# RWKV-7 attention with a SoLU block: wider inverse steps for the first six groups, narrower couplings, a new order for the first slots

## The chip, the cores and the metric

The kernel runs on one core of one Trainium2 chip, as one launch. The metric is the device time in microseconds (us). The core has five engines with a queue of instructions each: TensorE (PE in the profile, its weight loads PEld), VectorE (DVE), ScalarE (ACT), GpSimd (POOL) and SyncE (SP), which only issues transfers.

## The reference

```python
# attention: r, k, v, w, a, b are [4, 8, 768, 40]
state = zeros(B, H, 40, 40)
for t in range(768):
    y[:, :, t] = einsum('bhd,bhde->bhe', r_t, state)
    Sa = einsum('bhde,bhe->bhd', state, a_t)
    state = state * w_t[:, :, None, :] - einsum('bhd,bhe->bhde', Sa, b_t) + einsum('bhd,bhe->bhde', v_t, k_t)
x = y.transpose(0, 2, 1, 3).reshape(3072, 320)
# block: w_in [320, 1024], w_out [1024, 320] (float64), g_ln [1024]
h = x @ w_in
e = exp(h - max(h)); sm = e / (sum(e) + 1e-9)
solu = h * sm
out = ((solu - mean(solu)) / sqrt(var(solu) + 1e-6) * g_ln) @ w_out
```

All of it is float32 in the kernel; the float64 weights are taken apart by bit operations on the chip.

## The kernel before

The sequence is cut into 12 chunks of 64 tokens, and the four batches into two pairs, which makes 24 slots (slot i is pair i % 2 of chunk i // 2). In a slot the recurrence is solved in closed form: within a chunk every token depends on earlier ones through a strictly triangular 64 x 64 matrix per head, one for each of 16 heads of a pair. This matrix is cut in two halves of 32 (Q = 32). Its two diagonal 32 x 32 blocks are inverted on VectorE; the block off the diagonal is put together from these by two rounds of small products on TensorE, the coupling and the closing.

The steps of a slot, with the names that stand in the order list:

- w, b, a, k, v, r load the inputs (names with the slot's number). lg, Tc, xi, xe, sb, sk scale them with the running decay; sb and sk are VectorE's instructions "kb". Ta, Tb, Tk, Tv, Tr, Tei are transposes on TensorE, Ea, Eb, Ekv, Er, Eei their evictions (Ea is VectorE's "aT").
- N builds the triangular matrices, nt evicts them, sn stores their diagonal blocks to DRAM.
- Z, B, i: the inversion, done for two slots at once (GRP = 2), so there are 12 groups. B brings 64 blocks (two slots by two halves by 16 heads) onto 128 partitions as the tile blk, each block twice, for two sets of 16 columns. The pieces i0.1 to i0.30 are the 30 steps j of group 0: step j adds row j of blk, times column j of the result uu, to the columns behind it. U stores uu to DRAM, tu and uh bring the two diagonal inverses of a slot into the tiles tu and uh.
- F flips a tile, C (coupling) multiplies by the off-diagonal matrix nt, wy is its eviction, D (closing) multiplies by uh, and tl evicts the result into the tile tu.
- Sk, Sv, mk, mv are scores and their masks; K, V and x0 build the right side from the state, S solves with tu, clu and mlu evict and mask it as lu. R0, R1 read the answers; t, ks, an keep the state and write the answer x; lv and l move x through DRAM into xT, for h two slots later.
- H0 to H4 are h = x @ w_in, m the row maximum (the tile nmax), e, we, sq, rs the softmax and the norm, Te and Ee a transpose, P, Pr, Eo and So the product with w_out and its store.
- nb, ns, nf split the float64 weights in three stages (13 pieces: 5 of w_in, 8 of w_out), L lands them, g loads g_ln, and Tmean0 to Tmean2 with "centre" take the mean out of w_out.

An inverse step before (lines 548 to 564) depends on j. n_c = (j + 1) // 2 columns are live, and m = 31 - j elements are behind. For n_c under 4 there is one scalar_tensor_tensor per column (line 552). Else the columns are split in two halves, and the engine gets product, product (line 560), sum, sum (line 563).

The work is recorded as named pieces in a program order, and then sorted by the list ORDER. An engine runs its instructions strictly in the sorted order and waits for semaphores where an input comes from elsewhere. Pieces that the list does not name follow in program order; the list before names those up to about slot 10. From there on each slot is the same, and the coupling C comes behind the fourth piece of h.

Of the kernel before, what the change touches and what calls it, by code (L numbers as in the profile page):

```python
# [9 lines left out]
FP32 = mybir.dt.float32  # L10
# [15 lines left out]
NK = 5  # L26
FIRST = 6
# [4 lines left out]
w0 b0 b1 w1 a0 lg0 Tc0 xi0 xe0 Tei0 sb0 Tb0 Ta0 L1 lg1 Tc1 Eei0 Ea0 v0 Eb0 xi1 xe1 N0 nt0 Tei1 Eei1 sb1 Tb1 a1 Ta1 Ea1  # L32
L0 Eb1 N1 nt1 w2 lg2 a2 Tc2 nb0 k0 Z0 sn0 nb1 ns1 nf1 sn1q sk0 ns0 nf0 sn1 w3 xe2 b2 Z1 Ta2 xi2 B0 Tei2 Eei2 r0 Ea2
lg3 Tc3 xi3 k1 sb2 i0.1 i0.2 i0.3 i0.4 i0.5 i0.6 Tb2 Eb2 i0.7 i0.8 xe3 Tei3 Eei3 i0.9 i0.10 i0.11 i0.12 w4 N2 nt2 a3
Ta3 b3 b4 b5 i0.13 i0.14 w5 lg4 Tc4 xi4 xe4 sb3 Tb3 i0.15 i0.16 sn2 i0.17 i0.18 Tk0 cv0 Tv0 Ekv0 Tei4 K0 Ea3 Eb3 N3 a4
i0.19 L2 i0.20 i0.21 i0.22 i0.23 i0.24 i0.25 sb4 i0.26 i0.27 lg5 cr0 Tr0 nt3 Er0 i0.28 L3 Tc5 xe5 i0.29 i0.30 Eei4 sn3
a5 Tei5 Ta4 Ea4 v1 nb2 nb3 r1 ns3 Sv0 Sk0 mk0 mv0 V0 ns2 cv1 sk1 Eei5 nf3 nf2 B1 i1.1 i1.2 i1.3 x0.0 Ta5 xi5 sb5 Tb4
i1.4 i1.5 i1.6 i1.7 U0 i1.8 i1.9 i1.10 i1.11 cr1 Tv1 r2 Eb4 L4 nb4 Tk1 Ekv1 Tr1 Er1 cr2 Sk1 mk1 tu0 F0 N4 nt4 k2 i1.12
i1.13 i1.14 C0 sk2 g ns4 K1 wy0 i1.15 i1.16 uh0 i1.17 i1.18 D0 tu1 Sv1 mv1 w6 tl0 S0 lg6 Tc6 F1 Ea5 mlu0 V1 i1.19
i1.20 i1.21 k3 sk3 i1.22 i1.23 uh1 xi6 xe6 L5 nb5 clu0 R0.0 R1.0 an0 Tb5 Eb5 x0.1 Tei6 Eei6 Tg ks0 a7 v2 a6 Ta6 L6 L7  # L40
w7 Eg Tr2 N5 cv2 Tv2 Er2 b6 nt5 L8 i1.24 i1.25 i1.26 i1.27 i1.28 Tk2 Ekv2 i1.29 i1.30 lv0 C1 wy1 Sv2 ns5 D1 tl1 Ea6
nf4 nb6 Sk2 mk2 mv2 Ts2 sn5 S1 mlu1 nf5 nb7 Z2 lg7 Tc7 Es2 Sr2 ns6 Esr2 R0.1 K2 nf6 U1 xi7 sb6 clu1 nb8 R1.1 an1 sn4
l0 H0.0 ks1 ns7 nf7 xe7 Tei7 ns8 nf8 b7 Tb6 Eb6 Eei7 Ta7 Ea7 r3 cr3 B2 i2.1 i2.2 i2.3 i2.4 H0.1 i2.5 i2.6 i2.7 i2.8 V2
# [1353 lines left out]
```

## Time and profile before

| | us |
|---|---|
| median of 3 runs | 534.18 (533.07 to 534.34) |
| the profiled execution | 535.16 |
| its span, first to last instruction | 533.3 |

| engine | busy us | share of the span |
|---|---|---|
| TensorE products | 487.6 | 91% |
| TensorE weight loads | 394.7 | 74% |
| VectorE | 420.0 | 79% |
| ScalarE | 313.1 | 59% |
| GpSimd | 180.2 | 34% |

The profile has one line for every group of instructions: line of the kernel, engine, operation, output and inputs by the tiles' names, shape, count, then busy us, mean ns of one, and the idle time ahead of them with what ended it. In the timeline a row gives the start, the time from the first start to the last end of a row's instructions, and their count. Instructions on one engine can overlap, so starts tell more than sums. A windows row gives, after the stretch and its length, the busy us of PE, PEld, DVE, ACT and POOL, each with a count, then the granted clock, the share of the transfer engines and GB/s. TensorE makes two instructions of each float32 product, so a set of 16 products counts 32.

### The profile page before, as it was taken

What the parts mean: (1) busy time and instruction counts of PE and PEld (TensorE: products, weight loads), DVE (VectorE), ACT (ScalarE), POOL (GpSimd) and SP (SyncE); (2) the same over time, 40 slices, a digit from 0 to 9 for tenths busy, and PEclk for the clock granted to TensorE, in tenths of its full rate; (3) what the DMA queues carried; (4) which work ended last, traced back from release to release, by engine and by line L of the source; (5) the groups of instructions that cost most, each with busy time, mean ns of one, the idle gap of its engine ahead of it and who ended that gap; (6) DMA issues with size and microseconds to landing.
All of it is one profiled execution on the core that took longest, in us unless ns stands there. A gap on an engine that the chain in (4) does not pass through costs nothing.

```text
span 533.3 us, 28056 instructions
## 1 busy us (share of the span) xinstructions
PE 487.6 (91%) x12029; PEld 394.7 (74%) x12029; DVE 420.0 (79%) x1800; ACT 313.1 (59%) x627; POOL 180.2 (34%) x328
## 2 busy tenths in 40 slices
PE   4457589898999999999999999999999999999997
PEld 3345476666888877877888788788778877887766
DVE  5589988998998988879789879879979888544322
ACT  3546457785856655745766665566556655664433
POOL 3543237224434242533053343334252421210300
PEclk9999988998999999999999999999999999999999
DMA  9997679846666778766266675676554551420210
GB/s 155 171 185 149 150 140 187 189 95 118 133 134 129 131 154 142 150 142 141 48 135 117 124 163 100 116 152 123 105 120 95 109 115 43 103 68 27 62 53 25
DMA packets 194475, 63.95 MB, mean 120 GB/s; under 512 B 166840, under 2 KB 186528, under 8 KB 194352
## 3 DMA queue, kind: packets, MB, share of 16 engines
q1 hardware_dynamic: 181232, 41.60, 42.3%
q0 software_dynamic: 10768, 19.95, 15.8%
q8 instruction: 94, 1.54, 1.3%
q10 hardware_dynamic: 2352, 0.62, 0.7%
q14 instruction: 29, 0.24, 0.1%
HBM read 47.96 MB, written 14.16 MB: 116 GB/s over the span
## 4 chain that ended last, share of the span: by engine, by line
PE 77%; DMA 8%; DVE 7%; ACT 3%; SPq 3%; issue 2%; DVEq 0%; ACTq 0%
PE po L318 19%; PE h L318 18%; PE py L318 6%; PE pyo L318 6%; PE px L318 6%; PE ps L318 4%; PE pu L318 3%; DMA a<-in_a_dram 3%; PE plnT L883 2%; PE pkv L435 2%; PE psr L318 2%; PE pb L435 2%; PE pa L435 2%; SPq L344 2%; DVE prod L560 1%
## 5 line engine op out<-in xcount | busy, mean ns | idle before, releaser
L318 PE MATMUL h<-w_in,xT 64*64 64x512 f32 (+1 forms) x1064 | 122.2, 551 | 0.4 <-issue 0.2
L318 PE MATMUL po<-w,lnT 128*128 128x160 f32 x768 | 114.7, 304 | 0.0
L318 PEld LDWEIGHTS po<-w,lnT 128*128 128x128 f32 x768 | 105.4, 190 | 4.6 <-issue 0.8
L560 DVE TENSOR_TENSOR prod<-blk,uu 128x48 f32<-128x48 f32 (+19 forms) x576 | 93.9, 204 | 1.2
L563 DVE TENSOR_TENSOR uu<-uu,prod 128x48 f32<-128x48 f32 (+19 forms) x576 | 94.2, 204 | 0.0
L525 POOL DMA_DIRECT2D nt_dram<-nt x86 | 50.1, 590 | 110.9 <-ACT nt L513 109.6
L318 PEld LDWEIGHTS h<-w_in,xT 64*64 64x64 f32 x1064 | 38.9, 133 | 24.9 <-issue 20.6
L834 DVE TENSOR_REDUCE nmax<-h 128x1 f32<-128x1024 f32 x24 | 29.3, 1221 | 32.1 <-PE h L318 31.5
L871 POOL TENSOR_TENSOR rs<-var,mhalf 128x1 f32<-128x1 f32 x24 | 13.7, 571 | 119.4 <-ACT var L863 119.1
L344 POOL DMA_DIRECT2D raw_r<-in_r_dram x48 | 33.0, 692 | 26.5 <-ACT r L379 24.5
L862 ACT ACTIVATE sq<-e,mu 128x1024 f32<-128x1024 f32 x24 | 26.9, 1120 | 19.9 <-DVE e L850 19.9
L479 DVE TENSOR_TENSOR lu<-pu,cst 128x512 f32<-128x512 f32 x24 | 16.5, 687 | 27.0 <-PE pu L318 27.0
L842 ACT ACTIVATE e<-h,nmax 128x1024 f32<-128x1024 f32 x24 | 26.7, 1110 | 17.5 <-DVE nmax L834 17.3
L850 DVE SCALAR_TENSOR_TENSOR e<-h,e 128x1024 f32<-128x1024 f32 x24 | 29.3, 1221 | 5.4 <-ACT e L842 5.2
L602 ACT ACTIVATE wy<-py,cst 128x256 f32<-128x256 f32 x24 | 11.4, 474 | 37.4 <-PE py L318 37.4
L802 POOL DMA_DIRECT2D x_dram<-x x24 | 18.0, 750 | 37.9 <-DVE x L793 37.7
L552 DVE SCALAR_TENSOR_TENSOR uu<-blk,uu 128x30 f32<-128x30 f32 (+3 forms) x144 | 26.9, 242 | 2.5 <-DMA blk<-nt_dram 1.9
L665 ACT COPY st<-psr 128x416 f32<-128x416 f32 (+1 forms) x44 | 14.2, 377 | 24.7 <-PE psr L318 24.7
L629 ACT COPY kvT<-pkv 104x1024 f32<-104x1024 f32 x24 | 24.2, 1010 | 6.7 <-PE pkv L435 6.4
L318 PEld LDWEIGHTS py<-tu,nt 64*64 64x64 f32 x768 | 16.3, 141 | 14.2 <-issue 7.6
L318 PE MATMUL pu<-x,tu 64*64 64x104 f32 x768 | 25.9, 265 | 0.7 <-ACT bT L445 0.5
L318 PE MATMUL px<-lv,psi 64*64 64x104 f32 x768 | 24.2, 264 | 2.2 <-DVE lv L479 2.2
(154 smaller groups left out, 1067.5 us busy)
## 6 DMA issues: line engine op xcount, KB each, us to landing
xT<-x_dram SPq DMA_DIRECT2D x48, 160.0 KB, 3.9
blk<-nt_dram POOLq DMA_DIRECT2D x22, 256.0 KB, 4.8
raw_w<-in_w_dram SPq DMA_DIRECT2D x48, 80.0 KB, 3.7
lv<-in_v_dram SPq DMA_DIRECT2D x48, 80.0 KB, 3.1
raw_r<-in_r_dram POOLq DMA_DIRECT2D x48, 80.0 KB, 3.6
out_dram<-osb SPq DMA_DIRECT2D x46, 80.0 KB, 3.8
a<-in_a_dram SPq DMA_DIRECT2D x44, 80.0 KB, 3.7
raw_k<-in_k_dram SPq DMA_DIRECT2D x42, 80.0 KB, 3.4
```

Source lines behind the costliest of these rows:

```text
L318: nc.tensor.matmul(o, lhsT=lhsT, rhs=rhs, start=start, stop=stop, skip_group_check=True)
L344: queue.dma_start(out=x[half(p), :, 0:D], in_=ap[2 * bp + p, :, ci * C:(ci + 1) * C, :].rearrange("h t d -> t h d"))
L435: nc.tensor.transpose(out=t[0:W2, p, at + C * j:at + C * j + C], in_=x[half(p), 2 * j:2 * j + 2].rearrange("p a b -> p (a b)")[:, skip:ski ...
L525: queue.dma_start(out=blocks[n][e].rearrange("(a x h) s c -> a x s h c", a=GRP, x=2)[at, x], in_=nt[home:home + Q].rearrange("p h j c -> p ...
L552: nc.vector.scalar_tensor_tensor(out=u[:, c, j + 1:Q], in0=nb[:, j, j + 1:Q], scalar=u[:, c, j:j + 1], in1=u[:, c, j + 1:Q], op0=ALU.mult, ...
L560: nc.vector.tensor_tensor(out=ts[-1], in0=nb[:, j:j + 1, j + 1:Q].to_broadcast([P, hi - lo, m]), in1=u[:, lo:hi, j:j + 1].to_broadcast([P, ...
L563: nc.vector.tensor_tensor(out=u[:, lo:hi, j + 1:Q], in0=u[:, lo:hi, j + 1:Q], in1=x, op=ALU.add)
L629: return lambda: nc.scalar.copy(out=o[0:W2].rearrange("p b j t -> p b (j t)"), in_=t[0:W2])
L834: nc.vector.tensor_reduce(out=nmax, in_=d["h"], axis=AX.X, op=ALU.max, negate=True)
L842: nc.scalar.activation(out=e, in_=d["h"], func=AF.Exp, bias=d["nmax"], accum_out=d["esum"])
L850: nc.vector.scalar_tensor_tensor(out=d["e"], in0=d["h"], scalar=1.0 / DFF, in1=d["e"], op0=ALU.mult, op1=ALU.mult, accum_out=d["mu"])
L862: nc.scalar.activation(out=pair("A" if i == N - 2 else "h", "sq").rearrange("p a b -> p (a b)"), in_=d["e"], func=AF.Square, scale=-float( ...
```

## The change

- For groups 0 to 5 (WIDE = 6) a step does all its live columns at once: one product and one sum, where n_c is over 1. The two are pieces of their own, i and j, which the order list places one by one. The other six groups stay as they were.
- The coupling loads 33 of 64 weight columns (NARROW = 33) and fills 33 partitions. Before, rows 0 to 31 of the result were cleared by a scale and an identity block was kept in wy to pass the second inverse through the closing. Now the second inverse comes straight from DRAM into tu (the new piece ut, two transfers per slot), uh carries half as much, and the closing too works on 33 rows and 33 columns. Each of the two evictions becomes two instructions, one per half of the partitions.
- g is loaded through GpSimd's queue and no longer through ScalarE's.
- In program order the coupling goes ahead of the fourth piece of h instead of behind it.
- ORDER is a new list. It names pieces up to about slot 12.

The diff without most of the list ORDER; of the old and the new list the stretches around group 0 stand here.

```diff
+NARROW = Q + 1
+WIDE = 6
...
 ORDER = """
-w0 b0 b1 w1 a0 lg0 Tc0 xi0 xe0 Tei0 sb0 Tb0 Ta0 L1 lg1 Tc1 Eei0 Ea0 v0 Eb0 xi1 xe1 N0 nt0 Tei1 Eei1 sb1 Tb1 a1 Ta1 Ea1
-L0 Eb1 N1 nt1 w2 lg2 a2 Tc2 nb0 k0 Z0 sn0 nb1 ns1 nf1 sn1q sk0 ns0 nf0 sn1 w3 xe2 b2 Z1 Ta2 xi2 B0 Tei2 Eei2 r0 Ea2
-lg3 Tc3 xi3 k1 sb2 i0.1 i0.2 i0.3 i0.4 i0.5 i0.6 Tb2 Eb2 i0.7 i0.8 xe3 Tei3 Eei3 i0.9 i0.10 i0.11 i0.12 w4 N2 nt2 a3
...
+w0 b0 b1 lg0 Tc0 xi0 xe0 sb0 w1 K1 lg1 Tc1 xi1 sb1 Tei0 a0 Eei0 Ta0 Ea0 L0 a1 w2 Tb0 xe1 Tei1 Eb0 N0 k0 k1 sk0 nt0 Tb1
+Ta1 k2 b2 Eei1 Ea1 Eb1 N1 Z0 nb0 L1 lg2 nt1 r0 cr0 Tc2 xe2 Tei2 xi2 sb2 nb1 ns1 nf1 sk1 b3 sk2 sn0 sn1q sn1 w3 lg3 Tb2
+B0 i0.1 Tc3 Eei2 xi3 i0.2 b4 b5 i0.3 a2 xe3 j0.3 i0.4 j0.4 i0.5 j0.5 i0.6 j0.6 i0.7 j0.7 Eb2 g Ta2 Ea2 N2 i0.8 j0.8
...
+j0.24 i0.25 j0.25 i0.26 j0.26 Tei4 xe5 Tei5 Eei4 Eei5 nf0 nb2 ns2 nb3 i0.27 j0.27 Ta4 Ea4 xi5 i0.28 j0.28 Sk0 mk0
+i0.29 Ta5 j0.29 Tr1 ns3 Sv0 Er1 cr2 L4 i0.30 j0.30 U0 w6 a7 cv1 i1.1 i1.2 k3 i1.3 j1.3 i1.4 j1.4 N4 tu0 ut0 K0 mv0 V0
...
+D0 tl0 S0 nb4 i1.19 j1.19 clu0 R0.0 mlu0 R1.0 mv1 mk1 ns4 V1 x0.1 i1.20 j1.20 ks0 i1.21 Z2 sn4 v2 w7 w8 Tc6 an0 lv0
...
@@ -84,8 +102,6 @@
         ident=np.eye(P),
         cum=same & (s <= t),
         tri=row < np.arange(C)[None, :],
-        eye_hi=row == Q + np.arange(Q)[None, :],
-        hi=(row >= Q).astype(np.float64),
         mean=np.full((P, P), 2.0 ** -10),
     )
     at, where = 0, {}
@@ -173,11 +189,10 @@
     r_t = zeroed(nc.gpsimd, "r", [P, H, C], 1, pad)
     st_t = zeroed(nc.vector, "st", [P, 2, 8, C], NPAIR)
     tu_t = zeroed(nc.vector, "tu", [P, H, 3 * Q], 2)
-    uh_t = zeroed(nc.vector, "uh", [P, 2 * H, Q], 2)
+    uh_t = zeroed(nc.vector, "uh", [P, H, Q], 2)
     x0 = const.tile([P, 2, 4, W2], FP32, name="x0")
-    wy = const.tile([P, 2, 4, C], FP32, name="wy")
-    nc.vector.tensor_copy(out=wy.rearrange("p h j c -> p (h j) c")[:, :, Q:],
-                          in_=c_("eye_hi").unsqueeze(1).to_broadcast([P, 8, Q]))
+    wy = const.tile([P, 2, 4, NARROW], FP32, name="wy")
+    nc.vector.memset(wy[:, :, :, Q:], 0.0)
     above = const.tile([C, Q // 2, Q], FP32, name="above")
     nc.gpsimd.memset(above, 1.0)
     for x in range(Q // 2):
@@ -545,6 +560,22 @@
         flat = u.rearrange("p c t -> p (c t)")
         nc.vector.tensor_tensor(out=u[0:C], in0=nb[0:C, 0::2], in1=above, op=ALU.mult)
         nc.vector.memset(flat[0:C, 0::Q + 2], 1.0)
+        for j in range(1, (Q - 1) * (n < WIDE)):
+            m, n_c = Q - 1 - j, (j + 1) // 2
+            if n_c == 1:
+                nc.vector.scalar_tensor_tensor(out=u[:, 0, j + 1:Q], in0=nb[:, j, j + 1:Q], scalar=u[:, 0, j:j + 1],
+                                               in1=u[:, 0, j + 1:Q], op0=ALU.mult, op1=ALU.add)
+                yield
+                continue
+            prod = two.tile([P, P], FP32, tag=f"wide{n % 2}", name=f"wide{n % 2}", bufs=1)[:, 0:n_c * m]
+            x = prod.rearrange("p (c r) -> p c r", c=n_c)
+            nc.vector.tensor_tensor(out=x, in0=nb[:, j:j + 1, j + 1:Q].to_broadcast([P, n_c, m]),
+                                    in1=u[:, 0:n_c, j:j + 1].to_broadcast([P, n_c, m]), op=ALU.mult)
+            yield
+            nc.vector.tensor_tensor(out=u[:, 0:n_c, j + 1:Q], in0=u[:, 0:n_c, j + 1:Q], in1=x, op=ALU.add)
+            yield
+        if n < WIDE:
+            return
         for j in range(1, Q - 1):
             m, n_c = Q - 1 - j, (j + 1) // 2
             if n_c < 4:
@@ -581,7 +612,10 @@
             queue = nc.sync if i or not x else nc.gpsimd
             queue.dma_start(out=d["tu"][C * x:C * x + Q, :, Q:2 * Q], in_=src[0, at, :, x])
         for x in range(2 * (which == "u")):
-            nc.sync.dma_start(out=d["uh"][C * x + Q:C * x + C], in_=src[1, at].rearrange("c x h t -> c (x h) t"))
+            nc.sync.dma_start(out=d["uh"][C * x + 1:C * x + 1 + Q].rearrange("c (x h) t -> c x h t", x=2),
+                              in_=src[1, at][:, :, 4 * x:4 * x + 4])
+        for x in range(2 * (which == "v")):
+            nc.sync.dma_start(out=d["tu"][C * x + Q:C * x + C, :, 2 * Q:], in_=src[1, at, :, x])
 
     def flip(i):
         if not ok(i):
@@ -598,9 +632,13 @@
             p, q, g, h = u
             j = 2 * q + g
             x = half(p ^ h)
-            mm(t[half(p), h, j * Q:j * Q + Q], d["nt"][x, p, j], d["tu"][x, 4 * p + j, 0:Q])
-        return lambda: nc.scalar.activation(out=wy[:, :, :, 0:Q], in_=t[:, :, 0:4 * Q].rearrange("p h (j c) -> p h j c", j=4),
-                             func=AF.Copy, scale=c_("hi"))
+            mm(t[C * p:C * p + NARROW, h, j * Q:j * Q + Q], d["nt"][x, p, j, C - NARROW:], d["tu"][x, 4 * p + j, 0:Q])
+
+        def evict():
+            for p in range(2):
+                at = slice(C * p, C * p + NARROW)
+                nc.scalar.copy(out=wy[at, :, :, 0:Q], in_=t[at, :, 0:4 * Q].rearrange("p h (j c) -> p h j c", j=4))
+        return evict
 
     def close(i):
         if not ok(i):
@@ -610,9 +648,15 @@
         for u in in_turn(lambda p, q, g, h: (p, p ^ h)):
             p, q, g, h = u
             j = 2 * q + g
-            mm(t[half(p ^ h), p, 384 + j * Q:384 + j * Q + Q], wy[half(p), h, j], d["uh"][half(p), H * (p ^ h) + 4 * p + j])
-        return lambda: nc.scalar.copy(out=d["tu"].rearrange("p (h j) c -> p h j c", h=2)[:, :, :, 2 * Q:],
-                       in_=t[:, :, 384:].rearrange("p h (j c) -> p h j c", j=4))
+            y, z = p ^ h, slice(C * p, C * p + NARROW)
+            mm(t[C * y:C * y + NARROW, p, 384 + j * Q:384 + j * Q + Q], wy[z, h, j], d["uh"][z, 4 * y + j])
+
+        def evict():
+            for y in range(2):
+                at = slice(C * y, C * y + Q)
+                nc.scalar.copy(out=d["tu"][at].rearrange("p (h j) c -> p h j c", h=2)[:, :, :, 2 * Q:],
+                               in_=t[at, :, 384:].rearrange("p h (j c) -> p h j c", j=4))
+        return evict
 
 
     def attend_kv(i, t, which):
@@ -949,7 +993,7 @@
     def stepped(n):
         if n not in stepping:
             stepping[n] = invert(n)
-        next(stepping[n])
+        next(stepping[n], None)
 
     def lazily(tag, name):
         box = []
@@ -964,6 +1008,8 @@
         while due and due[0][0] <= last and n:
             x, left_ = due[0]
             do(f"i{x}.{Q - 1 - left_}", stepped, x)
+            if x < WIDE and Q - 1 - left_ > 2:
+                do(f"j{x}.{Q - 1 - left_}", stepped, x)
             n -= 1
             due[0][1] -= 1
             if not due[0][1]:
@@ -1041,6 +1087,7 @@
         if ok(i):
             do(f"tu{i}", bring, i, "t")
             do(f"uh{i}", bring, i, "u")
+            do(f"ut{i}", bring, i, "v")
 
     def xy(i):
         return "BC" if i < EARLY - AHEAD else ("BC", "CB")[(i - EARLY + AHEAD) % 2]
@@ -1053,7 +1100,7 @@
         keys(i, "w")
         keys(i, "b", nc.scalar)
         keys(i, "a")
-    do("g", lambda: nc.scalar.dma_start(out=g_rows, in_=moe_g_ln.rearrange("(c p) -> c p", p=P)))
+    do("g", lambda: nc.gpsimd.dma_start(out=g_rows, in_=moe_g_ln.rearrange("(c p) -> c p", p=P)))
     logged_(0)
     keys(2, "w")
     for n in range(2):
@@ -1290,9 +1337,9 @@
         ahead = 2 + (i >= EARLY - AHEAD)
         logged_(j + ahead)
         vector(plan[2], i)
-        run(6)
         if ok(i + 1):
             evict(f"wy{i + 1}", do_pe(f"C{i + 1}", lambda i=i: couple(i + 1)))
+        run(6)
         if i == LAG + 1:
             do("centre", lambda: centred(mean["mean2"]))
         run(7)
```

91 lines of the change are left out of this document (52 added, 39 removed).

## The prediction

> **What bounds the kernel now.** I read the page first (engine shares, the span in 40 slices), then the busy time of the engines by stage, then the waits of VectorE, then single groups and the timeline where a step needs a price.
>
> ```profile
> span 533.3 us, 28056 instructions
> PE 487.6 (91%) x12029; PEld 394.7 (74%) x12029; DVE 420.0 (79%) x1800; ACT 313.1 (59%) x627; POOL 180.2 (34%) x328
> ...
> PE   4457589898999999999999999999999999999997
> ...
> DVE  5589988998998988879789879879979888544322
> ```
>
> PE is busy for 91% of the span, and what it lacks lies in the first ten of 40 slices (its digits 4 to 8), where DVE stands at 8 and 9. The same by stage, columns PE, PEld, DVE, ACT, POOL:
>
> ```profile
> 26.60:40.00 13.40, 7.25 (x104) 5.72 (x108) 11.72 (x74) 5.60 (x12) 5.40 (x8) 1.00 1.15 186
> 53.30:66.60 13.30, 7.44 (x205) 6.62 (x202) 13.11 (x72) 5.94 (x11) 3.89 (x7) 1.00 0.64 150
> 80.00:106.60 26.60, 23.09 (x610) 16.82 (x605) 23.77 (x87) 19.29 (x41) 13.35 (x23) 0.94 0.93 188
> 133.00:200.00 67.00, 65.58 (x1703) 55.85 (x1698) 62.80 (x285) 42.74 (x89) 24.82 (x44) 1.00 0.69 136
> 200.00:300.00 100.00, 98.88 (x2660) 81.57 (x2660) 83.96 (x368) 61.78 (x125) 35.56 (x61) 1.00 0.63 125
> ```
>
> From 26.6 to 133 us DVE is the bound: 13.11 of 13.30 us in one stretch, 23.77 of 26.60 in another, with PE at 7.44 and 23.09. From 133 to 200 both are full (65.58 and 62.80 of 67), and from 200 on PE alone (98.88 of 100; DVE 83.96). So an edit that shortens DVE's queue pays before about 200 us, an edit that shortens PE pays behind 133 us, and one that shortens DVE later pays nothing.
>
> **Inverse groups by wide steps.** One group is 12 scalar_tensor_tensor and 96 tensor_tensor instructions; the changed one has 2 and 56. The prices:
>
> ```profile
> L560 DVE TENSOR_TENSOR prod<-blk,uu 128x60 f32<-128x60 f32 x84 | 15.1, 215 | 0.4
> L782 DVE TENSOR_TENSOR st<-tot,ex 104x160 f32<-104x160 f32 x40 | 11.1, 320 | 0.1
> L428 DVE TENSOR_TENSOR kb<-raw_b,inv 128x320 f32<-128x320 f32 x24 | 11.4, 474 | 4.7 <-ACT inv L398 2.5 <-DMA raw_b<-in_b_dram 2.2
> L462 DVE TENSOR_TENSOR aT<-pa,ex 104x512 f32<-104x512 f32 x18 | 12.4, 690 | 11.0 <-PE pa L435 10.7
> ```
>
> ```profile
> 29.40 2.23 DVE L552 SCALAR_TENSOR_TENSOR uu<-blk,uu 128x30 f32<-128x30 f32 x12
> 31.55 0.33 DVE L560 TENSOR_TENSOR prod<-blk,uu 128x48 f32<-128x48 f32 x2
> 31.79 0.33 DVE L563 TENSOR_TENSOR uu<-uu,prod 128x48 f32<-128x48 f32 x2
> ...
> 33.30 0.34 DVE L563 TENSOR_TENSOR uu<-uu,prod 128x42 f32<-128x42 f32 x2
> 33.68 0.35 DVE L560 TENSOR_TENSOR prod<-blk,uu 128x60 f32<-128x60 f32 x2
> ...
> 45.15 0.69 DVE L462 TENSOR_TENSOR aT<-pb,ex 104x512 f32<-104x512 f32 x1
> ```
>
> A product of 60 elements lasts 215 ns, one of 160 lasts 320, one of 320 some 474: about 1.05 ns an element over 152. Its slot in the queue is shorter than its duration. The two products at 31.55 end at 31.88, but the sums start at 31.79: an instruction whose inputs are ready starts some 0.085 us before the one ahead ends. Where the next needs the very last result, it starts behind it: the two sums at 33.30 end at 33.64 and the product that reads the second one starts at 33.68, 0.035 us later. So a dependence with nothing between costs 0.12 us. The halves of the old code hide that: product, product, sum, sum. Group 0 runs from 29.40 to 45.15, 15.75 us, with two kb and one aT in it (2 x 0.39 and 0.60 us of queue): 14.3 us of its own.
>
> The wide code has product, sum, product, sum, each needing the one ahead. Its 28 wide steps hold 2541 elements, 91 a piece: 152 + 95 = 247 ns, in the queue 0.163 us. With the two first (0.25) that is 56 x 0.163 + 2 x 0.17 = 9.4 us, plus 0.12 for each of 57 places that nothing fills. In the written order of the changed kernel 50, 40 and 40 places of groups 0, 1 and 2 have the group's own next instruction right behind, and the other 7, 17 and 17 some kb, aT, mask or weight step. So the groups cost 15.4, 14.2 and 14.2 us against 14.3: **+0.9** in all. The bounds are 9.4 (all filled) and 16.2 us (none): -14.7 to +5.7 over three groups. Groups 3 to 5 have 45, 49 and 47 such places; they stand where PE is full, and cost nothing as long as DVE keeps the 16 us per 100 that it has free.
>
> **What stands ahead of group 0.** The weight step nf0 moves from before group 0 to behind its step 26:
>
> ```profile
> 22.31 0.69 DVE L251 SCALAR_TENSOR_TENSOR w<-w,scale 128x512 int32<-128x512 int32 x1
> ...
> 24.24 0.68 DVE L462 TENSOR_TENSOR aT<-pa,ex 104x512 f32<-104x512 f32 x1
> ...
> 28.59 0.68 DVE L546 TENSOR_TENSOR uu<-blk,above 64x512 f32<-64x512 f32 x1 [0.99 <-DMA blk<-nt_dram]
> ```
>
> ```profile
> 23.02 1.11 SPq L534 DMA_DIRECT2D blk<-nt_dram  x2
> ```
>
> It took 22.31 to 24.24, 1.9 us, in time in which DVE waited anyway, since group 0 starts when blk lands (start 28.59, asked for at 23.02). On SP that request is the 27th and 28th transfer before and after the change (k1 and b3 come ahead of it, v0 and a2 go behind), so group 0 starts where it did. Two kb (0.39 each) and no aT (0.60) stand ahead of it instead, so DVE carries 1.9 - 0.8 + 0.6 = **+1.7 us** more through the stretch that binds. Bounds 0 and +1.9.
>
> **Idle time of DVE that the new order can fill.**
>
> ```profile
> DVE kb L428 <- DMA raw_b<-in_b_dram: 2.2, 1, 2.2
> DVE w L297 <- ACT mean L292: 2.0, 1, 2.0
> DVE aT L462 <- PE pa L435: 2.0, 2, 1.6
> DVE psi L479 <- PE ps L318: 1.5, 2, 1.2
> DVE nmax L834 <- PE h L318: 1.3, 1, 1.3
> DVE bits L251 <- ACT scale L243: 1.0, 1, 1.0
> DVE lu L479 <- PE pu L318: 0.9, 1, 0.9
> ```
>
> From 26 to 200 us DVE waits 10.9 us in these rows. The first 2.2 lie ahead of group 0, and blk would take their place. Of the other 8.7 us each is a wait of a piece for PE or ACT, with inverse steps queued behind it. The new order puts steps in front: two halves of step 19 between S0 and the mask of lu, steps 28 and 29 around Sk0 and its mask, splits into i and j that can be dealt out singly. Beside these rows lie gaps under the rows' size, before each change from one kind of work to another. I take **-6.5 us**; the bounds are 0 and -8.7. This is the weakest term: it is a judgement on an order, not a price.
>
> **Couplings.** They load 33 weight columns for 64, for the same number of products.
>
> ```profile
> 250.61 0.62 PE L318 MATMUL py<-tu,nt 64*64 64x32 f32 x32
> 251.04 1.07 PE L318 MATMUL h<-w_in,xT 64*64 64x512 f32 x12
> 251.93 0.62 PE L318 MATMUL py<-uh,wy 64*64 64x32 f32 x32
> ```
>
> ```profile
> 265.60 0.65 PE L318 MATMUL py<-aT,bT 40*64 40x64 f32 x32
> 266.07 0.90 PE L318 MATMUL px<-st,aT 40*64 40x104 f32 x32
> ```
>
> ```profile
> L318 PEld LDWEIGHTS py<-tu,nt 64*64 64x64 f32 x768 | 16.3, 141 | 14.2 <-issue 7.6 <-ACT scale L242 4.1 <-ACT nt L513 1.3
> L883 PEld LDWEIGHTS plnT<-cst,e 64*128 64x128 f32 x368 | 13.2, 138 | 3.5 <-ACT kvT L629 1.9 <-issue 1.3 <-ACT osb L931 0.2
> L435 PEld LDWEIGHTS pb<-cst,r 64*104 64x104 f32 x192 | 7.5, 132 | 1.9 <-ACT x L728 0.8 <-ACT ei L394 0.8
> ```
>
> 32 products of 32 moved columns take 0.62 us, of 64 columns 0.65, of 104 columns 0.90. So the moved columns do not set the coupling's time; either the weight columns do or the count of instructions. A load of 64 columns lasts 141 ns, of 104 columns 132, of 128 columns 138: the duration does not follow the columns, so I take the count, which stays: **0**. The other end is rival 2. There is no loss above 0, as no instruction is added on PE.
>
> Each eviction becomes two, one for each half of the partitions:
>
> ```profile
> L602 ACT ACTIVATE wy<-py,cst 128x256 f32<-128x256 f32 x24 | 11.4, 474 | 37.4 <-PE py L318 37.4
> L614 ACT COPY tu<-py 128x256 f32<-128x256 f32 x24 | 8.9, 371 | 23.6 <-PE py L318 23.6
> ```
>
> A copy of 256 columns lasts 0.37 us whatever its partitions; two in a row some 0.62 (the second starts about 0.12 before the first ends). That is +0.15 at wy (474 ns now) and +0.25 at tl, between coupling, closing and solving. In the steady stage it is hidden: the closing at 251.93 starts when the last h products end, and the change moves one more h piece (0.86 us) between coupling and closing. In the first two slots nothing covers it: **+0.8 us** at most on a chain that DVE binds; I take +0.4.
>
> The ut transfers (two per slot on SP, some 0.4 us each to issue) take over what uh carried; solving needs them only after the closing. uh itself halves. The g transfer leaves ACT's queue for GpSimd's. Cover for both is the wait for VectorE in the first slots; I take 0, and 0.8 us for each of three slots if ut is late.
>
> **Sum.** 535.2 (the profiled execution, span 533.3) + 0.9 + 1.7 - 6.5 + 0.4 = 531.7. The median of the runs (534.2) is 1.0 under the profiled one, so 530.7 us.
>
> **The rivals.**
>
> 1. Slower: the stalls of the wide steps are paid and the idle time is not won. DVE binds until about 200 us, so what its queue gains in length ends up in the time: +0.9 + 1.7, and groups 3 and 4, which still lie before 200 us, at 45 and 49 open places 0.5 and 1.0 us; nmax of slot 0, ahead of everything that frees h for slot 1, stands behind step 17 of group 2 instead of 14, three steps of some 0.5 us: with +0.4 for ACT, 6.0 us. It decides if 2 us of idle or less is won: 2 us won leaves 535.2 + 4.0 - 1.0 = 538.2. For it speak that the dependence is certain and that 62.80 of 67 us are full; against it, that what stands behind is not all needed at once.
>
> 2. Faster, by weight columns: if the loads set the 0.62 us, of which 0.14 is the last load's own length, the other 0.48 becomes 0.48 x 33/64, 0.23 less. 48 couplings on a full PE: -11 us, 520 with the forecast's other terms. For it speaks that 16 loads of 128 columns and 32 of 64 both come out near 0.6 us; against it the equal durations above. The Trainium skill, TensorE: Matmul & The Clock Gate, section LDWEIGHTS (loading the stationary operand), says the same in general: a load takes the columns over 1.2 GHz, whatever the rows. By that estimate 64 columns are 53 ns and 33 are 28; the trace's 132 ns for 104 columns beside 141 for 64 does not follow it, and no run here has 33.
>
> 3. No change: idle won and stalls paid cancel (won 3 us): 534.2.
>
> **How the numbers follow.** The forecast has 0.40, rival 1 0.34, rival 2 0.19, rival 3 0.07. Under 0.3% (1.6 us) a measurement of this kernel can't tell from no change. The forecast's own range is 526 to 533: faster but for a tenth. Faster is 0.38 + 0.19 = 0.57, the same 0.09, slower 0.34. The range takes in rival 2 at 520 and rival 1 with ut late in two slots (538.2 + 1.6): 519 to 540.
>
> **What the profile after would show.** Wide products of some 91 elements at about 247 ns, and starts 0.28 us apart where nothing stands between; group 0 at 28 to 29 us and its end near 51 us (with nf0, nb2, nb3, three aT and two kb in it). VectorE's waits from 26 to 200 us down by 6 us if the forecast holds, as now if rival 1 does; the first nmax, now at 100.8 us, tells which. 32 coupling products in 0.62 us, or 0.4 if rival 2 holds, at every slot to the end. A steady slot longer than now, or a wait of PE for tu or uh behind 133 us, would speak against all of these.

## The result and the profile after

The changed kernel takes **548.06 us** (median of 6 runs, 545.43 to 550.41), the kernel before 533.62 beside it (529.09 to 535.81): a ratio of **1.0285, interval 1.023 to 1.034**, 2.85% slower. Predicted were 530.7 us, in a range from 519 to 540. The profiled execution took 548.86. That of before, 535.16, lies at the upper end of its runs: beside the experiments the median before is 530.4 to 531.7. The ratios leave disturbed runs out and can differ a little from the quotient of two medians.

The page after, span, busy time, and the slices of TensorE and VectorE:

```profile
span 546.7 us, 27924 instructions
...
PE 487.3 (89%) x12029; PEld 394.0 (72%) x12029; DVE 416.7 (76%) x1500; ACT 328.5 (60%) x675; POOL 182.1 (33%) x329
...
PE   4456587879999989969999999999999999999997
...
DVE  4488999996998969947787898888979878634312
```

TensorE's work is the same (487.3 us for 487.6) in a span 13.4 us longer. By stage, in the stretches that the prediction read (columns PE, PEld, DVE, ACT, POOL):

```profile
26.60:40.00 13.40, 7.39 (x92) 5.89 (x96) 10.53 (x38) 6.09 (x13) 4.27 (x7) 1.00 1.24 170
53.30:66.60 13.30, 6.22 (x180) 5.12 (x176) 12.16 (x40) 4.80 (x11) 3.30 (x5) 1.00 0.88 151
80.00:106.60 26.60, 21.14 (x570) 14.54 (x564) 24.57 (x79) 19.43 (x42) 7.49 (x13) 0.94 0.77 156
133.00:200.00 67.00, 62.31 (x1688) 51.65 (x1684) 60.92 (x181) 42.40 (x90) 23.89 (x39) 1.00 0.57 110
200.00:300.00 100.00, 93.00 (x2396) 76.13 (x2388) 74.69 (x265) 59.54 (x125) 31.29 (x54) 0.97 0.66 126
```

TensorE does less in four of the five (6.22 for 7.44, 21.14 for 23.09, 62.31 for 65.58, 93.00 for 98.88), and VectorE is not fuller but emptier in three of these four, by 9.3 us from 200 to 300. By these rows no engine has become fuller all through: they wait for each other more. A part of what VectorE lost is the 0.03 to 0.04 us by which a dependent wide step starts behind the end of the one ahead (rows further down), which is not counted as busy. Group 0 and the first row maximum; each pair of fences shows before, then after:

```profile
45.26 1.32 SPq L570 DMA_DIRECT2D uu_dram<-uu  x2
```

```profile
52.07 1.33 SPq L601 DMA_DIRECT2D uu_dram<-uu  x2
```

```profile
100.82 1.22 DVE L834 TENSOR_REDUCE nmax<-h 128x1 f32<-128x1024 f32 x1
```

```profile
107.24 1.22 DVE L878 TENSOR_REDUCE nmax<-h 128x1 f32<-128x1024 f32 x1
```

The first inverse leaves 6.8 us later, the first row maximum comes 6.4 us later. The difference between the two traces stays near 6 until the third (159.5 for 153.1), grows to 16 at the ninth (286.2 for 270.0), and is 14 at the end. The largest single wait of TensorE behind 200 us, then ScalarE's ahead of it, then SP's queue ahead of that:

```profile
241.69 0.68 PE L333 MATMUL py<-tu,nt 64*33 64x32 f32 x32 [4.77 <-ACT nt L528]
```

```profile
240.68 0.46 ACT L394 COPY v<-lv 128x320 f32<-128x320 f32 x1 [7.10 <-DMA lv<-in_v_dram]
241.05 0.59 ACT L528 ACTIVATE nt<-py 128x512 f32<-128x512 f32 x1
```

```profile
233.20 1.16 SPq L980 DMA_DIRECT2D out_dram<-osb  x2
234.53 1.29 SPq L856 DMA_DIRECT2D xT<-x_dram  x2
235.86 2.25 SPq L359 DMA_DIRECT2D lv<-in_v_dram  x2
```

By the trace the coupling (slot 9's) waits for an eviction nt, which stands on ScalarE behind the copy of v, and v waited 7.1 us for a load that stood on SP behind a store of the output. Before there is no such wait from 230 to 250 us. All of these are pieces that the new list names: it asks for this load (v10) one piece ahead of its copy (cv10), where the old list has 43 pieces between.

### The profile page after: what moved, and what is told of

Same layout as the page of the kernel before. It is cut to its first block, busy times and chain, and to the rows that moved or that the text cites. A ratio compares the mean times of both kernels' runs of the same rounds, so it can differ in the third digit from the quotient of the medians.

```text
span 546.7 us, 27924 instructions
## 1 busy us (share of the span) xinstructions
PE 487.3 (89%) x12029; PEld 394.0 (72%) x12029; DVE 416.7 (76%) x1500; ACT 328.5 (60%) x675; POOL 182.1 (33%) x329
## 4 chain that ended last, share of the span: by engine, by line
PE 68%; DVE 10%; DMA 9%; SPq 5%; issue 4%; ACT 3%; POOL 1%; DVEq 0%; POOLq 0%; ACTq 0%
PE po L333 18%; PE h L333 17%; PE px L333 6%; PE pyo L333 5%; PE py L333 4%; SPq L359 3%; PE ps L333 3%; PE pu L333 3%; DVE uu L575 2%; DMA blk<-nt_dram 2%; PE plnT L927 2%; DVE wide L572 2%; DMA nt_dram<-nt 2%; PE pkv L450 2%; PE psr L333 2%
## 5 line engine op out<-in xcount | busy, mean ns | idle before, releaser
L333 PEld LDWEIGHTS h<-w_in,xT 64*64 64x64 f32 x1064 | 43.3, 135 | 34.5 <-issue 31.5
L591 DVE TENSOR_TENSOR prod<-blk,uu 128x60 f32<-128x60 f32 (+28 forms) x288 | 46.7, 202 | 0.6
L594 DVE TENSOR_TENSOR uu<-uu,prod 128x60 f32<-128x60 f32 (+28 forms) x288 | 46.8, 202 | 0.0
L575 DVE TENSOR_TENSOR uu<-uu,wide 128x110 f32<-128x110 f32 (+19 forms) x168 | 42.2, 251 | 4.7
L572 DVE TENSOR_TENSOR wide<-blk,uu 128x110 f32<-128x110 f32 (+19 forms) x168 | 42.2, 251 | 4.5
L657 ACT COPY tu<-py 32x256 f32<-32x256 f32 x48 | 17.4, 362 | 33.3 <-PE py L333 31.6
L886 ACT ACTIVATE e<-h,nmax 128x1024 f32<-128x1024 f32 x24 | 26.6, 1110 | 16.1 <-DVE nmax L878 16.0
L640 ACT COPY wy<-py 33x256 f32<-33x256 f32 x48 | 17.6, 367 | 28.3 <-PE py L333 27.7
L815 DVE TENSOR_TENSOR tot<-pyo,st 104x416 f32<-104x416 f32 x44 | 24.1, 582 | 5.0 <-PE pyo L333 5.0
L333 PE MATMUL pcum<-lw,cst 128*128 128x160 f32 x48 | 14.8, 453 | 14.7 <-ACT lw L399 14.4
L333 PE MATMUL pyo<-lu,kb 64*64 64x104 f32 x768 | 24.0, 256 | 4.2 <-ACT lu L786 1.8
```

Source lines behind the costliest of these rows:

```text
L333: nc.tensor.matmul(o, lhsT=lhsT, rhs=rhs, start=start, stop=stop, skip_group_check=True)
L572: nc.vector.tensor_tensor(out=x, in0=nb[:, j:j + 1, j + 1:Q].to_broadcast([P, n_c, m]), in1=u[:, 0:n_c, j:j + 1].to_broadcast([P, n_c, m]) ...
L575: nc.vector.tensor_tensor(out=u[:, 0:n_c, j + 1:Q], in0=u[:, 0:n_c, j + 1:Q], in1=x, op=ALU.add)
L591: nc.vector.tensor_tensor(out=ts[-1], in0=nb[:, j:j + 1, j + 1:Q].to_broadcast([P, hi - lo, m]), in1=u[:, lo:hi, j:j + 1].to_broadcast([P, ...
L594: nc.vector.tensor_tensor(out=u[:, lo:hi, j + 1:Q], in0=u[:, lo:hi, j + 1:Q], in1=x, op=ALU.add)
L815: nc.vector.tensor_tensor(out=by_b(d["tot"])[:, :, :, part], in0=answers(i)[:, :, :, part], in1=by_b(state_of(i)[:, x])[:, :, :, 0:HW], op ...
```

## The experiments

### Which part of the change costs

Three theories. "Order": the new list holds work up in the queues. "Wide": the steps that wait for each other cost it. "Narrow": the couplings' added evictions and transfers cost it. Four kernels, each with a part of the change:

```diff
e1_old_order:    after, with the ORDER of before (j behind its i, ut behind uh)
e2_order_alone:  before, with the ORDER of after (j and ut dropped)
e3_narrow_alone: after, WIDE = 0, with the ORDER of before
e4_wide_alone:   before, + the wide steps (WIDE = 6, j behind its i)
```

Expected of e1:

> The changed kernel with the list ORDER of before; every second half j of a wide step stands right behind its first half i, and ut right behind uh. Theory 'order' (the 14 us are lost by the new list: queues in which a late transfer holds up what stands behind it): about 528 to 536 us, since only the wide steps (some 3 us either way) and the narrow couplings (48 a run, each 0.15 to 0.2 us shorter in the trace) are left. Theory 'wide' (the steps that wait for each other cost it): 543 to 555, more than the changed kernel, as now no step is spaced. Theory 'narrow' (more evictions and transfers cost it): 542 to 550.

Expected of e2:

> The kernel before with the new list alone: its steps, its couplings, its place of g. A whole step stands where the list has the first half. Theory 'order': 544 to 551 us. Theories 'wide' and 'narrow': 530 to 537, at or a little under the kernel before.

Expected of e3:

> The changed kernel without wide steps and with the list of before (ut right behind uh): the 33-column couplings, ut, g on GpSimd's queue and the later place of the fourth piece of h are what is left. Theories 'order' and 'wide': 525 to 532 us, the gain of 48 shorter couplings on a full TensorE, 0.15 us each or 7 us at most, less what else bounds a slot. Theory 'narrow': 542 to 550.

Expected of e4:

> The kernel before with wide steps in the first six groups, nothing spaced (j right behind i), the list of before. Theory 'order': 531 to 540 us (by the price of the steps, 9.4 + 57 x 0.12 = 16.2 us a group against 14.3, three groups that bind: up to 5.7 us more). Theory 'wide': 543 to 552. Theory 'narrow': 531 to 540.

| kernel | median us | ratio to before (531.11), interval |
|---|---|---|
| e1: wide and narrow, old list | 540.08 | 1.0157 (1.0111 to 1.0202) |
| e2: new list alone | 540.48 | 1.0175 (1.0131 to 1.0218) |
| e3: narrow alone | 533.89 | 1.0039 (1.0003 to 1.0074) |
| e4: wide alone | 534.99 | 1.0073 (1.0038 to 1.0107) |

No theory is right alone, and e1, e2 and e3 lie in no range that a theory had named. The three parts cost 1.75, 0.73 and 0.39%: order 9.4 us, wide 3.9, narrow 2 to 3. Together that is 2.87%, near the 2.85% of the whole, but the intervals are too wide to say that the parts simply add: wide and narrow are 1.12% by their sum and 1.57% in e1. The list is the largest single part, and nothing in the change pays. The granted clock is not what costs in e2: its runs at a clock of 0.991 and 0.993 took 540.86 and 541.79 us, those at 0.946 took 540.10 and 539.67.

The new list alone is also the plainest test of the prediction, as e2 has the same instructions as before. From 26 to 100 us and from 100 to 200, before and then e2:

```profile
26.00:100.00 74.00, 53.20 (x1217) 42.52 (x1216) 67.42 (x333) 42.21 (x87) 32.17 (x51) 0.95 0.87 169
100.00:200.00 100.00, 94.67 (x2469) 77.16 (x2471) 92.48 (x398) 65.79 (x136) 35.03 (x61) 0.98 0.66 129
```

```profile
26.00:100.00 74.00, 48.98 (x1058) 37.80 (x1059) 67.92 (x326) 42.01 (x86) 23.87 (x39) 0.77 0.90 168
100.00:200.00 100.00, 93.73 (x2597) 75.47 (x2595) 91.57 (x400) 64.98 (x134) 37.93 (x65) 1.00 0.63 122
```

VectorE is as busy as before (67.92 us for 67.42, then 91.57 for 92.48), and TensorE does 4.2 us less by 100 us (48.98 for 53.20). The same amount of VectorE's work, in another order, feeds TensorE later.

### Narrow couplings: what eats their gain

The couplings did get shorter. Groups from 300 to 480 us, before and after:

```profile
L318 PE MATMUL py<-uh,wy 64*64 64x32 f32 x320 | 7.0, 216 | 0.4 <-issue 0.2
...
L318 PEld LDWEIGHTS py<-tu,nt 64*64 64x64 f32 x320 | 6.7, 134 | 5.4 <-issue 4.6 <-DVE uu L563 0.3 <-ACT r L379 0.3
...
L318 PE MATMUL py<-tu,nt 64*64 64x32 f32 x320 | 6.2, 215 | 0.0
```

```profile
L333 PE MATMUL py<-uh,wy 33*33 33x32 f32 x320 | 5.5, 195 | 1.0 <-issue 1.0
...
L333 PE MATMUL py<-tu,nt 64*33 64x32 f32 x288 | 4.3, 194 | 0.0
...
L333 PEld LDWEIGHTS py<-tu,nt 64*33 64x33 f32 x288 | 4.1, 108 | 0.0
```

A coupling of 32 products fell from 6.2/10 = 0.62 us to 4.3/9 = 0.48, a closing from 0.70 to 0.55; a load of 33 columns lasts 108 ns, of 64 columns 134. Some 0.14 us for each of 48 couplings and closings: up to 7 us. Ten steady slots (row maximum 10 to 20) took 179.8 us before, 178.0 after, 177.6 in e3. Yet e3 as a whole is no faster. Five kernels on e3's base (e16 and e18 leave the second inverse out of the solution, so they are probes and no replacement):

```diff
e8:  the coupling behind run(6), as in before
e7:  - nc.sync.dma_start(out=d["tu"][C * x + Q:C * x + C, :, 2 * Q:], ...)
     + nc.gpsimd.dma_start(the same)
e16: - do(f"ut{i}", bring, i, "v")
e17: ut{i} behind wy{i} instead of behind uh{i}, from slot 2 on
e18: - nc.sync.dma_start(out=d["tu"][C * x + Q:C * x + C, :, 2 * Q:], in_=src[1, at, :, x])
     + nc.sync.dma_start(out=ux_t[i % 2][C * x + Q:C * x + C], in_=src[1, at, :, x])
```

Expected of e8:

> Narrow couplings alone (533.9 us), with the coupling behind the fourth piece of h again, as before. Traces of three kernels with narrow couplings had ten steady slots (row maximum 10 to 20) in 177.1 to 178.0 us, against 178.5 to 179.8 in five without. If the place of the coupling costs: 530 to 532. If it helps or does nothing: 533.5 to 536.

Expected of e7:

> The kernel with narrow couplings alone (533.9 us), but with the two ut transfers of each slot on GpSimd's queue and no longer on SP's, whose issues stood back to back from 195 to 224 us. Theory 'queue' (the couplings gain, and ut on SP gives it back by making loads late): 527 to 531. Theory 'nothing to gain' (a shorter coupling only leaves a longer wait behind it): 532 to 536. GpSimd can also be a worse place (it waits in order too): 536 or more.

Expected of e16:

> Narrow couplings alone (533.9 us) without the transfers ut: the second inverse is never brought into tu, so that half of the solution is left out, and two transfers a slot less stand on SP's queue. All instructions of the engines are the same. If ut costs what the narrow couplings lose: 527 to 531 us. If the doubled evictions cost it, or nothing is to be had: 533 to 535.

Expected of e17:

> Narrow couplings alone (533.9 us; without ut at all 529.2), with the transfers ut asked for later: from slot 2 on right behind the coupling's eviction wy, and no longer right behind uh, so that the loads that stood behind ut on SP's queue go ahead of it. Solving needs ut only 9 to 20 us after the coupling from slot 2 on. If ut costs by its place on SP's queue: 529 to 531 us, at or under the kernel before. If it costs as traffic, wherever it stands (on GpSimd's queue it was 535.0): 533 to 535.

Expected of e18:

> Narrow couplings alone (533.9 us; without ut 529.2), with the transfers ut of the same number, bytes and place on the queue, but landing in a tile of their own where eight heads lie next to each other, so that a row is one long piece and not eight pieces of 128 bytes. Nothing reads that tile: the second inverse is left out of the solution, as in the run without ut. If ut costs by its 13,000 small packets: 528 to 531 us. If it costs by the two issues a slot on SP, or by solving's wait for it: the issues alone would give 532 to 535, the wait 528 to 531 (this run can't tell a wait from packets).

| kernel | median us | ratio to before, interval |
|---|---|---|
| e8: coupling behind the fourth h | 533.78 | 1.0077 (1.0041 to 1.0112) |
| e7: ut on GpSimd's queue | 535.00 | 1.0085 (1.0043 to 1.0127) |
| e16: no ut | 529.16 | **0.9960 (0.9927 to 0.9994)** |
| e17: ut later on SP | 533.21 | 1.0050 (1.0013 to 1.0087) |
| e18: ut in long packets, not read | 533.17 | 1.0055 (1.0018 to 1.0092) |

Without ut the narrow couplings gain 0.4%; with it they lose 0.4 to 0.85, on either queue, early or late. It is not the small packets: e18 has 2,300 more than e16, e3 13,000 more, and e18 and e3 cost about the same (e16, e18, e3):

```profile
DMA packets 196027, 62.36 MB, mean 118 GB/s; under 512 B 166856, under 2 KB 189616, under 8 KB 195904
```

```profile
DMA packets 198331, 63.94 MB, mean 121 GB/s; under 512 B 167624, under 2 KB 191920, under 8 KB 198208
```

```profile
DMA packets 209084, 63.96 MB, mean 121 GB/s; under 512 B 179912, under 2 KB 202672, under 8 KB 208960
```

Nor is it solving's wait, since nothing reads ut in e18. Nor is it the doubled evictions, which e16 has too. What e18 has and e16 has not is two transfers a slot: their issues, some 0.42 us each on SP, and their 1.6 MB. Which of the two costs, and where in the run, is not shown: ten steady slots take 176.7 us in e16 and 177.1, 177.6 and 178.4 in e17, e3 and e18, less than 0.2 us a slot more, and that is not the whole. That GpSimd's queue was no better says that it was no free place either. Moving the coupling back (e8) does not help.

### The list: is it its head, its rest, or one place?

All on the kernel before. "Close": the new list spaces the steps of groups 0 and 1 by other work, so each group is closed late, and the couplings wait. "Sum": only the length of VectorE's queue counts, as the prediction had it.

```diff
e5:  new list up to F0, then the old sequence
e6:  old list up to F0, then the new sequence
e9:  new list; ns0 nf0 ahead of group 0; nb2 ns2 nb3 ns3 behind U0
e12: old list; i0.27 i0.28 i0.29 i0.30 behind mv0
e10: new list; i0.27 to i0.30 and U0 behind i0.26; tu0 uh0 ahead of w6; F0 behind i1.11
e11: e10; and i1.26 to i1.30 and U1 behind i1.25
```

Expected of e5:

> The kernel before, with the new list for all that the new list has ahead of the first flip F0 (about the first 63 us), and the old list's sequence for the rest. The new list alone took 540.5 us, the kernel before 531.1. Theory 'head' (group 0 is closed late: its result was stored at 45.3 us before and at 51.9 us with the new list, and the first slots hang on it): 537 to 542. Theory 'middle' (the later part holds up transfers): 529 to 534.

Expected of e6:

> The kernel before, with the old list for all that stands ahead of F0 there (about 60 us), and the new list's sequence for the rest. Theory 'head': 529 to 534 us; group 0 is stored near 45 us again. Theory 'middle': 537 to 542.

Expected of e9:

> The kernel before with the new list alone, but with the weight step nf0 (and ns0, which it needs) taken from inside group 0 to the place ahead of it, and nb2 ns2 nb3 ns3 from inside group 0 to the place behind its store U0. That takes 1.9 + 1.4 = 3.3 us of VectorE's work out of the stretch between the group's first and last step, and leaves the sum of its queue as it was. Theory 'head' (the lateness of group 0): U0 near 48.6 us for 51.9, the first row maximum some 3 us earlier, 536 to 538.5 us for 540.5. Theory 'sum' (VectorE's queue as a whole counts, as the prediction had it): nf0 falls into idle time ahead of group 0, 1.9 us at most, the rest nothing: 538.5 to 541.

Expected of e12:

> The kernel before, its own list, with one thing moved: the last four steps of group 0 (i0.27 to i0.30, 2 us of VectorE) behind the masks of slot 0 (mv0), that is behind one aT, two weight pieces and two masks, 3.2 us of work that stood behind them. VectorE's queue has the same length and the same work. Theory 'close' (the moment at which a group is closed sets when the next couplings can run, and TensorE stands idle till then): U0 at about 49 to 50 us for 45.3, first row maximum 3 to 5 us later, 533 to 536 us for 531. Theory 'sum' (only the length of VectorE's queue counts): 530 to 532, or a little faster, as the masks come earlier.

Expected of e10:

> The kernel before with the new list alone (540.5 us), in which slot 0's first part is put early again: i0.27 to i0.30 and U0 right behind i0.26, tu0 and uh0 ahead of the loads w6 and a7 on SP's queue, F0 behind i1.11 instead of i1.17. Theory 'close': U0 near 47.5 us for 51.9, first coupling near 59 for 63.8, TensorE's idle time from 30 to 60 us 3 to 5 us down, 535 to 538 us. If what counts is group 1 or something later: 539 to 541.

Expected of e11:

> As the kernel with slot 0 early, and the last five steps of group 1 with its store U1 taken ahead too, right behind i1.25 (they were spread over some 40 pieces). Theory 'close': U1 near 76 to 78 us for 83.2, couplings of slots 2 and 3 some 4 us earlier, the idle time of TensorE from 80 to 100 us down from 9.5 towards 4, 531 to 535 us. If closing early only pushes other work back: 538 to 542.

| kernel | median us | ratio to before, interval |
|---|---|---|
| e5: new head | 539.22 | 1.0183 (1.0135 to 1.0232) |
| e6: old head, new rest | 540.36 | 1.0186 (1.0123 to 1.0248) |
| e9: 3.3 us taken out of group 0 | 540.73 | 1.0198 (1.0144 to 1.0252) |
| e12: old list, group 0 closed late | 530.37 | 1.0020 (0.9981 to 1.0058) |
| e10: slot 0 early | 541.21 | 1.0211 (1.0167 to 1.0254) |
| e11: groups 0 and 1 early | 545.27 | 1.0305 (1.0260 to 1.0349) |

Either part of the new list costs as much as the whole. e12 came out as "sum" expected: group 0 was stored 4.3 us later and it cost nothing; the first row maximum even came earlier (97.85 us for 100.82). "Close" found no support, but no clean test either, since none of the moves carried through to the coupling that was meant to gain or lose by it: slot 0's coupling starts at 60.6 us before and 61.8 in e12, at 63.8 in e2, and at 65.0, 66.2 and 66.9 in e9, e10 and e11, which were to bring it ahead. e11 stored group 1 at 82.0 us where 76 to 78 was meant, and lost 4 us more than e10, beyond either range. The traces say why a single move fails. In e9 the 3.3 us taken out came back as a later start of group 0 (29.47 us for 28.27) and a longer wait inside it:

```profile
49.65 0.69 DVE L469 TENSOR_TENSOR aT<-pb,ex 104x512 f32<-104x512 f32 x1 [3.21 <-PE pb L442]
```

In e12 U0 left at 49.59, but tu0 stands on SP behind eight other transfers, and was issued little later than before (55.58 us, 54.16 before):

```profile
49.59 1.32 SPq L570 DMA_DIRECT2D uu_dram<-uu  x2
50.97 4.16 SPq L221 DMA_DIRECT2D w<-in_moe_w_in_dram  x8
55.58 0.32 SPq L582 DMA_DIRECT2D tu<-uu_dram  x1
```

In e10 U0 and tu0 went ahead as meant, but the load w6 then stood behind them, and the logarithm that needs it stands on ScalarE ahead of an eviction that TensorE needs before the coupling (SP, ScalarE, TensorE):

```profile
57.08 1.33 SPq L351 DMA_DIRECT2D raw_w<-in_w_dram  x2
```

```profile
63.84 0.47 ACT L391 ACTIVATE lw<-raw_w 128x320 f32<-128x320 f32 x1 [6.32 <-DMA raw_w<-in_w_dram]
64.21 0.99 ACT L636 COPY kvT<-pkv 104x1024 f32<-104x1024 f32 x1
```

```profile
65.26 1.14 PE L325 MATMUL ps<-aT,kvT 40*64 40x64 f32 x32 [7.09 <-ACT kvT L636]
66.16 1.03 PE L325 MATMUL py<-tu,nt 64*64 64x32 f32 x32
```

The first coupling starts at 66.16 us, where the new list untouched had it at 63.8.

One place in the list shows in two traces. The load v10 that was seen above, asked for one piece ahead of its copy, holds up ScalarE in e2 too: 4.6 us there and 7.1 in the changed kernel, with TensorE waiting 2.4 and 4.8 us behind it. No run moved this load alone, so what it is worth stays open.

### Whose sequence?

Theory "transfers": the sequence of SP and GpSimd costs it; "engines": that of the other three. The places of one set of pieces are taken from the new list, the others from the old.

```diff
e13: SP and GpSimd new;                 TensorE, VectorE, ScalarE old
e14: TensorE, VectorE, ScalarE new;     SP and GpSimd old
e15: TensorE and ScalarE new;           VectorE, SP and GpSimd old
```

Expected of e13:

> The kernel before, in whose list the pieces of SP and GpSimd (loads, stores, the transfers of the inverse and of xT, memsets) stand at the places of the new list, and all pieces of TensorE, VectorE and ScalarE in the old sequence (a piece is put off only where it needs data of another). Theory 'transfers' (a2 behind b4 and b5, w6 and a7 ahead of tu0 and the like make TensorE wait): 536 to 541 us, most of the 9.4. Theory 'engines' (the sequence on the engines costs it): 530 to 533.

Expected of e14:

> The other half: TensorE, VectorE and ScalarE in the new sequence, SP and GpSimd in the old. Theory 'transfers': 530 to 534 us. Theory 'engines': 537 to 541. If both halves cost 8 or more, each is fitted to the other, and any mixture loses.

Expected of e15:

> Only TensorE and ScalarE in the new sequence; VectorE, SP and GpSimd in the old. If VectorE's sequence (steps spread among other work) is what costs in the new list, this is 530 to 534 us while the run with all three engines new is 537 to 541; if TensorE's own sequence costs, both are 536 to 541.

| kernel | median us | ratio to before (530.51), interval |
|---|---|---|
| e13: transfers new | 551.88 | 1.0411 (1.0360 to 1.0462) |
| e14: three engines new | 558.29 | 1.0517 (1.0467 to 1.0567) |
| e15: TensorE and ScalarE new | 563.41 | 1.0590 (1.0527 to 1.0654) |

Each half alone costs 21 and 28 us, the whole new list 9.4. The third case of e14 came true (both halves cost 8 or more), and all three runs lie above every range that was named in us: the queues of one list are fitted to each other, and mixtures like these cannot put the loss down to one queue. The mixtures were put together by a rule and never fitted afterwards; how much of their 21 to 33 us that rule costs is not shown. What stays open is whether a longer search from the new list would bring it under the old one; the cost is shown, a single cause of it is not. No version tried here beats the kernel before and still computes all of the reference.

## Why the prediction was wrong

- **What bounds the kernel: the step behind the failure.** "From 26.6 to 133 us DVE is the bound" was read from how full VectorE's queue is, and the sum then counted every wait of that queue that is filled as time won. e2 shows that this step fails: VectorE was as busy as before up to 200 us, TensorE got its work later, and the time went up by 9.4 us. What the list changes is which of VectorE's work comes first and what stands between on the other queues, and neither shows in how full one queue is. That the length of VectorE's queue counts as well is not refuted: e12 kept the length and cost nothing. By the Trainium skill, Perfetto Trace Analysis, section Identifying the Most-Contended Engine, the engine with the highest occupancy is the one to optimize first; in the first stages that is VectorE, and no run here shortened its queue in the old order, so none tests that rule.
- **Idle time filled, -6.5 us: the step that failed.** The prediction called it the weakest term. VectorE's longest waits from 26 to 200 us in the changed kernel:

```profile
DVE aT L477 <- PE pb L450: 3.3, 1, 3.3
DVE uu L566 <- DMA blk<-nt_dram: 1.6, 4, 0.7
DVE e L894 <- ACT e L886: 1.4, 2, 1.0
DVE uu L561 <- DMA blk<-nt_dram: 1.3, 1, 1.3
DVE kb L443 <- ACT inv L413: 0.7, 1, 0.7
```

  All eight rows of that view add up to 9.4 us; before it has ten, 13.3 us, of which the prediction added up seven (10.9). So some 4 us of such waits did go (1.1 in e2, which has 12.2), and the time did not follow: the list alone cost +9.4 us where -6.5 was taken. Its work filled gaps of one engine and opened larger ones on the others, which the term did not ask about. The trace of the changed kernel shows one of them from the start: the transposes of a waited 3.7 us for their load from 30 to 62 us (0.7 before), since a2 is now asked for behind blk. The prediction had seen that a2 goes behind, and priced only what this does to blk.

```profile
PE pa L450 <- DMA a<-in_a_dram: 3.7, 2, 2.9
```

- **Wide steps, +0.9 us: the price of a step was right, the total is not shown to be.** Predicted were 247 ns a product and starts 0.28 us apart:

```profile
L572 DVE TENSOR_TENSOR wide<-blk,uu 128x110 f32<-128x110 f32 (+19 forms) x168 | 42.2, 251 | 4.5
```

```profile
36.61 0.29 DVE L572 TENSOR_TENSOR wide<-blk,uu 128x126 f32<-128x126 f32 x1
36.94 0.29 DVE L575 TENSOR_TENSOR uu<-uu,wide 128x126 f32<-128x126 f32 x1
```

  251 ns, and for 126 elements a duration of 0.29 and starts 0.33 apart, the 0.035 of the working included. Group 0 ended at 52.0, predicted near 51. With nothing spaced (e4) the wide steps cost 3.9 us; the bound for that was 5.7. No run has them spaced without the new list's cost.
- **nf0 moved, +1.7:** putting it ahead of group 0 again, and four more weight pieces behind it, won nothing (540.73 for 540.48).
- **Evictions, +0.4:** a pair lasted 0.74 us where some 0.62 was taken, but e16, which has all the doubled evictions, is no slower than the kernel before.
- **Couplings, 0: mis-sized.** The term was "the count of instructions"; the columns count too, 0.14 us a piece where rival 2 had 0.23. Rival 2's mechanism holds in part, and so does the rule it named: by the Trainium skill, TensorE: Matmul & The Clock Gate, section LDWEIGHTS (loading the stationary operand), a load takes its columns over 1.2 GHz, an estimate of 26 ns less for 33 columns than for 64. The trace has 26 ns less too (108 for 134), but each load lasts some 80 ns more than by the rule.
- **ut, 0: mis-sized.** The prediction covered two issues a slot by "the wait for VectorE in the first slots". They cost 4 to 5 us (533.89 with them, 529.16 without), more than the couplings won. That wait is one of the first slots, and they recur in all 24; where in the run they cost is not shown.
- **Rival 1** had the sign and a late first row maximum (6.4 us late), but not the place: it stopped at 200 us and 538.2 us. The trace loses 5.9 us more of TensorE's work from 200 to 300, 4.8 of it in the one wait at 241.69 behind a load that comes late. Nor does the first row maximum tell which case holds, as the prediction meant it to: in e12 it came 3 us earlier and the time was the same. The prediction's own test against all cases, "a wait of PE for tu or uh behind 133 us", came in another form, as that wait for nt. One slip lies in its chances: "faster but for a tenth" leaves 0.36 of the forecast's 0.40, and 0.38 was added up.

## What to carry to other kernels

An order that was fitted to a kernel is one object over all its queues: price a new one by what each moved transfer and eviction holds up on the *other* queues, and give a rewritten list a loss as its likeliest outcome, since here the new list, its repairs and its mixtures with the old lost 1.8 to 5.9%, and only a small move that left the transfers in place cost nothing (e12). That one queue is nearly full does not say that filling its waits shortens the kernel: in e2 VectorE stayed as busy and TensorE fell 4.2 us behind by 100 us. When an edit saves time on the busiest engine by adding transfers, count what they cost in every repetition before counting the saving.

## What the runs showed of the hardware

- Loads of 33 weight columns lasted 108 ns and of 64 columns 134 in the steady stretch, and sets of 32 small products 0.48 and 0.62 us: weight columns count even where 32 moved columns follow, at less than in proportion.
- Two more transfers in each of 24 slots made the kernel 4 to 6 us slower than without them (529.16 us), whether their packets were 128 bytes (533.89) or eight times that (533.17), and on SP's queue or GpSimd's (535.00).
- A dependent VectorE instruction started 0.03 to 0.04 us behind the end of the one ahead, with 126 elements (36.94 us behind 36.90) and with 15 (51.86 behind 51.82).
